# An attention tail in quarters of the array, and its sums in eight groups of rows or folded

## The chip, the cores and the metric

The kernel runs on one core of a Trainium2 chip. The metric is device time in microseconds (us) of one execution; the median of several runs is compared. A core has five engines with queues of their own: TensorE (PE; its weight loads are PEld), VectorE (DVE), ScalarE (ACT), GpSimd (POOL) and SyncE (SP), which here issues nearly all DMA transfers.

## The reference

Three blocks follow each other, over 4 sequences of 448 tokens and 768 channels. The first is attention with 12 heads of 64 channels and a soft cap of 30 on the scores:

```python
scores = cap * np.tanh(scale * q @ k.T / cap)          # 448 x 448 per head
scores = scores - np.max(scores, axis=-1, keepdims=True)
attn = np.exp(scores)
attn = attn / (np.sum(attn, axis=-1, keepdims=True) + 1e-09)
x = attn @ v
# second block, xk = mu_k * x + (1 - mu_k) * x_prev, xr likewise with mu_r
x = sigmoid(xr @ w_r) * (np.maximum(xk @ w_k, 0.0) ** 2 @ w_v)
# third block
theta = x @ w_theta
y = w_tok_r @ (x * np.cos(theta)) + w_tok_i @ (x * np.sin(theta))
u = x + y
return u + np.maximum(u @ w_ch, 0.0)
```

## The kernel before

The program has two copies of the body behind a branch on `cap`: with a cap under 64 the row maximum needs no subtraction, and this copy (`exact` false) is the one that runs. Attention goes over 24 pairs of heads (`g`), six to a sequence; the two heads of a pair lie in partitions 0 to 63 and 64 to 127. Matmuls of the weights (the second and third block) are split into three f16 matmuls of 448 columns each (high by high, high by low, low by high; lines 723 to 725, 897 to 899, 927 to 929, 949 to 951). Those of attention are f32, which the hardware runs as two records per matmul, each with a weight load of its own.

In `scores` the 448 keys of a head are taken in chunks of 128, 128, 128 and 64 (`c` = 0 to 3). For a full chunk four matmuls of 64 by 64 stand on the four quarters of the array (line 636), scores stand as keys by queries, and ScalarE makes tanh (642) and exp (646) of 896 columns, to a tile `th`. The last 64 keys of both heads are the tail: one matmul of the whole array (632) against `kd`, a 128 by 128 tile with the two heads' keys on its diagonal and zeros elsewhere, loaded by two small transfers (`diagonal`, 374); its exp is the tile `tl`, 448 columns.

In `attend` VectorE adds the three full chunks into `pz` (654). `sums` has eight matmuls of 224 columns against ones (661, 664) that put the denominators of the two heads and of the two halves of the queries into four strips of 32 rows of a PSUM tile; `den` takes the reciprocal of 224 columns (671); `spread` brings it back to 128 rows by 448 columns with two matmuls against `row` (676). `av` is the product with the values: one whole-array matmul for the tail against `vd`, values on a diagonal (680), and six of 64 columns of the array (683). ScalarE or VectorE copies it out of PSUM with a factor, VectorE multiplies by the reciprocals (688) and mixes with the token before (691 to 698), which gives the f16 operands of the next f16 matmuls.

The order on every engine is worked out ahead by a planner, `Plan.order`: a list schedule with a duration and a rank for each operation, buffers with a fixed number of slots, one queue per engine. Operations that can run on several engines carry a duration for each. At the start, `open1` makes the tiles and issues the first loads; the queries of pair 0 go on SP's queue (397), its keys on ScalarE's (398) behind the loads of `cap` and of `mu` (316, 322).

Of the kernel before, what the change touches and what calls it, by code (L numbers as in the profile page):

```python
# [7 lines left out]
F32 = mybir.dt.float32  # L8
# [12 lines left out]
NP = H // 2  # L21
# [3 lines left out]
SH = S // 2  # L25
KD = DM // 128
# [54 lines left out]
class Plan:  # L81
# [5 lines left out]
    COLS = {"av": 1.0}  # L87
    TICK = 10.24 / 3
# [58 lines left out]
    def order(self):  # L147
# [20 lines left out]
        tick, cols, warm = 0, 0.0, False  # L168
        while True:
            for e, h in ready.items():  # L170
# [81 lines left out]
def act(n):  # L252
    return 0.17 + n / 1150.0
# [19 lines left out]
def body(nc, tc, exact, qk, v, cap, mu_k, mu_r, w_k, w_v, w_r, w_th, w_tr, w_ti, w_ch, out):  # L273
# [3 lines left out]
    SLOT = 7.9  # L277
    WV0, WV1 = 190.0, 28.0
# [41 lines left out]
    mu = cpool.tile([128, 2, KD], F32, name="mu")  # L320
    for i, src in enumerate((mu_k, mu_r)):
# [3 lines left out]
    mgc = cpool.tile([128, 1], F32, name="mgc")  # L325
    nc.gpsimd.memset(mgc, MAGIC)
    unit = cpool.tile([128, 1], F32, name="unit")
    nc.gpsimd.memset(unit, 1.0)
    ones = cpool.tile([128, 3, 32], F32, name="ones")
    nc.gpsimd.memset(ones, 0.0)  # L330
    nc.gpsimd.memset(ones[:, 0], 1.0)
    nc.gpsimd.memset(ones[0:64, 1], 1.0)
    nc.gpsimd.memset(ones[64:128, 2], 1.0)
    row = cpool.tile([128, 2, 2, D], F32, name="row")
    nc.gpsimd.memset(row, 0.0)
    for h in range(2):
        for i in range(2):
            nc.gpsimd.memset(row[32 * (2 * h + i):32 * (2 * h + i) + 1, i, h], 1.0)
# [31 lines left out]
    def diagonal(e, t, src):  # L370

        for i in range(2):
            p = slice(64 * i, 64 * i + 64)
            e.dma_start(out=t[p, p], in_=src(p, i))

    def open1():
# [16 lines left out]
        qk_s.tiles = [(ra.tile([128, 2, S], F32, name=f"qk{i}"), ra.tile([128, 128], F32, name=f"kd{i}")) for i in range(qk_s.n)]  # L393
        vn_s.tiles = [(ra.tile([128, 2, KC, D], F32, name=f"vn{i}"), ra.tile([128, 128], F32, name=f"vd{i}")) for i in range(vn_s.n)]
        for _, t in qk_s.tiles + vn_s.tiles:
# [5 lines left out]
        tl_s.tiles = tiles(ra, tl_s.n, [128, S], F32, "tl")  # L401
        pz_s.tiles = tiles(ra, pz_s.n, [128, 2, S], F32, "pz")
        if exact:
            kr_s.tiles = tiles(ra, kr_s.n, [128, 2, S], F32R, "kr")
            mq_s.tiles = tiles(ra, mq_s.n, [KN, 2, 2 * KC], F32, "mq")
            mb_s.tiles = [(ra.tile([128, 2, S], F32, name=f"mb{i}"), ra.tile([128, S], F32, name=f"ml{i}")) for i in range(mb_s.n)]
        rs_s.tiles = tiles(ra, rs_s.n, [128, SH], F32, "rs")
        for t in xt_s.tiles:
            nc.gpsimd.memset(t[:, 0:1], 0.0)

    o_open1 = op("SYS", 2.0, 0, open1)
# [135 lines left out]
    tiny(3, lambda: nc.vector.tensor_scalar(out=fm.t, in0=mk.t, scalar1=-1.0, scalar2=1.0, op0=ALU.mult, op1=ALU.add), w=[fm])  # L547
    tiny(3, lambda: nc.vector.scalar_tensor_tensor(out=fa.t, in0=mk.t, scalar=-1.0, in1=mk.t, op0=ALU.mult, op1=ALU.max), w=[fa])
# [35 lines left out]
    def inputs(g):  # L584
        A = g * PAIR
        t = qkb[g] = Buf(qk_s)
        if g == 0:
            op("SYS", 3.0, A, lambda: None, w=[t], after=[o_open1], name="first")
        else:
            op("DMA", 1.3, A - 30, lambda: nc.sync.dma_start(out=t.t[0], in_=qk[g].rearrange("p (t s) -> p t s", t=2)), w=[(t, 0)], after=[o_open1], name="ldqk")  # L590
# [442 lines left out]
```

## Time and profile before

| | |
|---|---|
| median of 3 runs | 823.13 us (821.58 to 827.53) |
| the profiled execution | 822.97 us, its span in the trace 821.2 us |
| granted TensorE clock | 0.996 of full |
| TensorE busy | 791.1 us, 96% of the span |
| VectorE busy | 547.8 us, 67% |
| ScalarE busy | 439.1 us, 53% |
| GpSimd busy | 106.8 us, 13% |
| transfers | 114.73 MB, mean 140 GB/s |

Busy time of TensorE is counted from the start of a matmul to its modelled end, so it overlaps the next one's; how long a matmul holds the engine is read from the distance of two starts.

### The profile page before, as it was taken

The page shows a single profiled execution, that of the slowest core. Times are in us where ns is not written, and L with a number is a line of the kernel's source. Part 1 is how long each engine was busy: PE and PEld are TensorE (multiplying, and loading weights), DVE is VectorE, ACT ScalarE, POOL GpSimd, SP SyncE. Part 2 cuts the span into 40 slices and gives each one's busy share as a digit, 9 for nine tenths or more (in the row PEclk, how much of TensorE's full clock was granted, in tenths as well). Part 3 has the DMA queues.
Part 4 walks back from the last instruction along what each step waited for, and adds up shares of the span by engine and source line. Part 5 has one row for each costly group of instructions (what it writes and reads, how often), then busy time and mean ns, then how long its engine had stood idle before and what let it go on. Part 6 is the DMA issues. An engine that isn't in the chain of part 4 may idle for free. (4 is left out here: it accounts for less than half of the span.)

```text
span 821.2 us, 12133 instructions
## 1 busy us (share of the span) xinstructions
PE 791.1 (96%) x4586; PEld 382.0 (47%) x4586; DVE 547.8 (67%) x990; ACT 439.1 (53%) x661; POOL 106.8 (13%) x124
## 2 busy tenths in 40 slices
PE   3999999999999999999899998999999999999997
PEld 1343345444444444444455554555555555555553
DVE  1788998787666575776766877876865555545531
ACT  2898888668766666554553544444654323233201
POOL 1144223320011100111200010110401000000000
PEclk9999999999999999999999999999999999999999
DMA  6765455434533244132556887543635432434412
GB/s 207 244 197 170 154 189 196 152 125 147 165 124 127 73 137 149 49 100 75 179 174 224 289 251 235 168 145 91 136 68 108 117 81 75 93 72 98 97 38 72
DMA packets 119139, 114.73 MB, mean 140 GB/s; under 512 B 58144, under 2 KB 111136, under 8 KB 119072
## 3 DMA queue, kind: packets, MB, share of 16 engines
q1 hardware_dynamic: 117056, 113.60, 46.6%
q8 instruction: 38, 0.62, 0.3%
q10 hardware_dynamic: 2016, 0.27, 0.2%
q14 instruction: 29, 0.24, 0.1%
HBM read 78.98 MB, written 23.86 MB: 125 GB/s over the span
## 5 line engine op out<-in xcount | busy, mean ns | idle before, releaser
L642 ACT ACTIVATE th<-big,tsc 128x896 f32<-128x896 f32 x72 | 71.1, 1004 | 32.6 <-PE big L636 31.7
L646 ACT ACTIVATE th<-th,cap_t 128x896 f32<-128x896 f32 x72 | 74.1, 1040 | 0.6
L636 PE MATMUL big<-qk 64*64 64x448 f32 x576 | 70.4, 569 | 1.3 <-ACT th L642 0.8
L723 PE MATMUL one<-k,wv 128*128 128x448 f16 x192 | 68.3, 356 | 3.1 <-DVE scal L505 2.3
L723 PE MATMUL one<-sl,wk 128*128 128x448 f16 x192 | 67.9, 354 | 2.9 <-ACT g L734 2.9
L725 PE MATMUL one<-k,wv 128*128 128x448 f16 x192 | 68.3, 356 | 0.0
L724 PE MATMUL one<-k,wv 128*128 128x448 f16 x192 | 68.3, 356 | 0.0
L725 PE MATMUL one<-sl,wk 128*128 128x448 f16 x192 | 67.7, 352 | 0.0
L724 PE MATMUL one<-sl,wk 128*128 128x448 f16 x192 | 67.6, 352 | 0.0
L683 PE MATMUL one<-th,vn 128*64 128x448 f32 x288 | 59.4, 548 | 0.0
L928 PE MATMUL q<-wo,zt 128*128 128x448 f16 x168 | 59.2, 352 | 0.0
L929 PE MATMUL q<-wo,zt 128*128 128x448 f16 x168 | 59.2, 352 | 0.0
L927 PE MATMUL q<-wo,zt 128*128 128x448 f16 x168 | 59.2, 352 | 0.0
L953 ACT ACTIVATE z<-one,scal 128x448 f32<-128x448 f32 x24 | 15.1, 628 | 71.7 <-PE one L951 71.7
L698 POOL TENSOR_TENSOR sl<-mx,sl 128x448 f16<-128x448 f32 x32 | 38.5, 1206 | 99.9 <-ACT sl L288 98.2
L723 PE MATMUL one<-sl,wr 128*128 128x448 f16 x144 | 51.0, 354 | 0.0
L725 PE MATMUL one<-sl,wr 128*128 128x448 f16 x144 | 50.7, 352 | 0.0
L724 PE MATMUL one<-sl,wr 128*128 128x448 f16 x144 | 50.7, 352 | 0.0
L913 DVE SCALAR_TENSOR_TENSOR cs<-xf,scal,cs 128x896 f32<-128x896 f32 x24 | 27.6, 1150 | 30.4 <-DMA xf<-xd 24.3
L671 DVE RECIPROCAL rs<-one 128x224 f32<-128x224 f32 x24 | 37.3, 1555 | 8.9 <-PE one L664 8.6
L954 DVE TENSOR_TENSOR xf<-z,xf 128x448 f32<-128x448 f32 x24 | 15.0, 624 | 35.0 <-ACT z L953 35.0
L949 PE MATMUL one<-w_u,wc 128*128 128x448 f16 x108 | 38.1, 352 | 0.0
(182 smaller groups left out, 1674.3 us busy)
## 6 DMA issues: line engine op xcount, KB each, us to landing
qk<-in_qk SPq DMA_DIRECT2D x23, 448.0 KB, 3.5
kd<-g SPq DMA_DIRECT2D x32, 224.0 KB, 2.6
vn<-in_v SPq DMA_DIRECT2D x24, 256.0 KB, 2.8
w<-in_v SPq DMA_DIRECT2D x8, 768.0 KB, 4.6
w<-in_w_k SPq DMA_DIRECT2D x8, 768.0 KB, 5.4
w<-in_w_v SPq DMA_DIRECT2D x12, 512.0 KB, 3.8
zd<-tmp SPq DMA_DIRECT2D x24, 224.0 KB, 2.0
z<-zd SPq DMA_DIRECT2D x24, 224.0 KB, 3.2
```

The costliest lines, as they stand in the source:

```text
L636: nc.tensor.matmul(ps.t[o, h, 0:S], t.t[0][p, 1, 128 * c + 64 * i:128 * c + 64 * i + 64], t.t[0][p, 0], start=True, stop=True)
L642: op("ACT", act(n * S) + 0.08, A + 1 + 1.8 * c, lambda src=src, th=th: nc.scalar.activation(out=th.t, in_=src(), func=AF.Tanh, scale=tsc), ...
L646: op("ACT", act(n * S) + 0.08, A + 3 + 1.8 * c, lambda th=th: nc.scalar.activation(out=th.t, in_=th.t, func=AF.Exp, scale=cap_t), w=[th], ...
L683: nc.tensor.matmul(ps.t[64 * h:64 * h + 64, 0:S], vn.t[0][:, h, c], th[c].t[:, h], start=False, stop=(c == 2), skip_group_check=True)
L698: op(tt(S, True), 0, R + i, lambda e, t=t, hi=hi, lo=lo: e.tensor_tensor(out=lo.t, in0=t.t, in1=hi.t, op=ALU.subtract), r=[t, hi], w=[lo], ...
L723: nc.tensor.matmul(ps.t[:, 0:S], wh, xh(), start=(kk == 0), stop=False)
L724: nc.tensor.matmul(ps.t[:, 0:S], wh, xl(), start=False, stop=False)
L725: nc.tensor.matmul(ps.t[:, 0:S], wl, xh(), start=False, stop=(kk == len(xs) - 1))
L927: nc.tensor.matmul(o, z.t[:, 0, i], wo[i].t[:, 0], start=(i == 0), stop=False)
L928: nc.tensor.matmul(o, z.t[:, 1, i], wo[i].t[:, 0], start=False, stop=False)
L929: nc.tensor.matmul(o, z.t[:, 0, i], wo[i].t[:, 1], start=False, stop=(i == KT - 1))
L949: nc.tensor.matmul(ps.t[:, 0:S], wh, u.t[:, 0], start=(kk == 0), stop=False)
```

## The change

It has six parts.

1. The tail of the scores is four matmuls of 64 by 64 on the quarters of the array, 224 queries each; the tile `tl` then holds keys and half of the queries in its partitions, 2 heads by 224 columns. `kd` and its transfers are gone. `vd` holds the values of one half of the queries' partitions with zeros in the other, and the tail's part of `av` is four matmuls of 64 columns of the array, behind the six others.
2. For pairs under `WIDE` = 12 (`narrow`), the sums lie in eight groups of 16 rows: sixteen matmuls of 112 columns, a reciprocal of 112 columns, four spread matmuls of 112 columns.
3. For pairs from 12 on (`wide`), two additions of 64 rows (`fold`, on VectorE or POOL) put the tail into `pz`, two matmuls against ones give the sums on all 128 rows by 448 columns, the reciprocal is taken of all of these, and one operation multiplies the product, the factor and the reciprocal.
4. At the start both halves of pair 0 are issued on SP's queue, `mu` is loaded as 12 rows and turned by a matmul against the identity, a tanh of one column loads ScalarE's table early, and the fill of `kd` and `row` on POOL gives way to eight copies on VectorE.
5. The planner counts 0.09 us for each step of TensorE into or out of "qk", "av" and "sums", its estimates for these are new, and the opening operations count 1 us less each. So the whole order is made anew.
6. The copy with the row maximum changes likewise; it doesn't run here.

```diff
+    MODE = {"qk": 1, "av": 2, "sums": 3}
...
+                if e == "PE" and mode != (m := self.MODE.get(got.name, 0)):
+                    got.dur += 0.09 * ((m > 0) + (mode > 0))
+                    mode = m
...
     for i, src in enumerate((mu_k, mu_r)):
-        nc.scalar.dma_start(out=mu[:, i], in_=src.rearrange("(j p) -> p j", p=128))
+        nc.scalar.dma_start(out=mut[KD * i:KD * i + KD], in_=src.rearrange("(j p) -> j p", p=128))
...
+    nc.scalar.activation(out=warm, in_=hpi, func=AF.Tanh)
...
-        nc.sync.dma_start(out=qk_s.tiles[0][0][:, 0], in_=qk[0][:, 0:S])
-        nc.scalar.dma_start(out=qk_s.tiles[0][0][:, 1], in_=qk[0][:, S:2 * S])
-        diagonal(nc.scalar, qk_s.tiles[0][1], lambda p, i: qk[0][p, S + 384:2 * S])
+        for i in range(2):
+            nc.sync.dma_start(out=qk_s.tiles[0][:, i], in_=qk[0][:, S * i:S * i + S])
...
                 if c == 3:
-                    nc.tensor.matmul(ps.t[:, 0, 0:S], t.t[1], t.t[0][:, 0], start=True, stop=True)
+                    for h, i in ((0, 0), (1, 0), (0, 1), (1, 1)):
+                        p = slice(64 * h, 64 * h + 64)
+                        nc.tensor.matmul(ps.t[64 * i:64 * i + 64, h, 0:SH], t.t[p, 1, 384:S], t.t[p, 0, SH * i:SH * i + SH], start=True, stop=True)
...
+    def narrow(A, x, sxb, th, vn, z, sp, rs, ps):
+        def sums():
+            for k in range(2):
+                for h, i in ((0, 0), (0, 1), (1, 0), (1, 1)):
+                    c, q = 32 * (2 * h + i), SH * i + SQ * k
+                    nc.tensor.matmul(sp.t[c:c + 32, 0:SQ], ones[:, 0, k], z.t[:, h, q:q + SQ], start=(k == 0), stop=False)
+            for k in range(2):
+                for h, i in ((0, 0), (0, 1), (1, 0), (1, 1)):
+                    c = 32 * (2 * h + i)
+                    nc.tensor.matmul(sp.t[c:c + 32, 0:SQ], ones[:, 1 + i, k], th[3].t[:, h, SQ * k:SQ * k + SQ], start=False, stop=(k == 1))
...
+            nc.vector.reciprocal(out=rs.t, in_=rs.t if exact else sp.t[:, 0:SQ])
...
+            for i in range(4):
+                nc.tensor.matmul(sp.t[:, SQ * i:SQ * i + SQ], live["row"][:, i].rearrange("p h d -> p (h d)"), rs.t, start=True, stop=True)
...
+            for i in range(2):
+                for h in range(2):
+                    nc.tensor.matmul(ps.t[64 * h:64 * h + 64, SH * i:SH * i + SH], vn.t[1][:, i, h], th[3].t[:, h], start=False, stop=True, skip_group_check=True)
...
+    def wide(A, x, sxb, th, vn, z, sp, ps):
+        rs = lambda: x.t[:, 1:S + 1]
+        def sums():
+            for h in range(2):
+                nc.tensor.matmul(sp.t[64 * h:64 * h + 64, 0:S], unit.to_broadcast([128, D]), z.t[:, h], start=True, stop=True, skip_group_check=True)
...
+            nc.vector.reciprocal(out=rs(), in_=rs() if exact else sp.t[:, 0:S])
...
+            out=x.t[:, 1:S + 1], in0=ps.t[:, 0:S], scalar=sxb.t, in1=rs(), op0=ALU.mult, op1=ALU.mult), r=[ps, sxb], w=[x], name="norm"))
...
+        if g >= WIDE:
             for i in range(2):
+                p, q = slice(64 * i, 64 * i + 64), slice(SH * i, SH * i + SH)
+                op(tt(S), 0, A - 1 + 0.5 * i, lambda e, p=p, q=q: e.tensor_tensor(out=z.t[p, :, q], in0=z.t[p, :, q], in1=th[3].t[p], op=ALU.add), r=[th[3]], w=[(z, i)], name="fold")
+            wide(A, x, sx[b], th, vn, z, sp, ps)
+        else:
+            narrow(A, x, sx[b], th, vn, z, sp, rs, ps)
```

What stands on the queues is shown at three places. The first is TensorE at the very start (`big` are the PSUM tiles of the scores, `qk` the queries and keys, `one` other PSUM tiles, `w` the loaded values whose size is measured). Before:

```order
L421 MATMUL one_201<-ident,scal 128x128
L636 MATMUL big_205<-qk_266 64x448 x4
L636 MATMUL big_206<-qk_266 64x448 x4
L480 LDWEIGHTS w_228
L480 MATMUL one_201<-w_228 128x128
```

After:

```order
L651 MATMUL big_203<-qk_264 64x448 x4
L651 MATMUL big_204<-qk_264 64x448 x4
L551 MATMUL one_199<-ident,mut 128x12
L651 MATMUL big_203<-qk_264 64x448 x4
L482 LDWEIGHTS w_226
L482 MATMUL one_199<-w_226 128x128
```

The matmul that belongs to `mu` (421, now 551) moved from ahead of the first scores to behind two groups of them, and a third group stands ahead of the matmuls on `w`.

The second place is TensorE at the first pair's sums and product, with the next pair's scores around them. Before:

```order
L680 MATMUL one_198<-tl_299,vd_275 128x448
L683 MATMUL one_198<-th_291,vn_274 64x448 x2
L683 MATMUL one_198<-th_292,vn_274 64x448 x2
L683 MATMUL one_198<-th_293,vn_274 64x448 x2
L661 MATMUL one_201<-pz_302,ones 32x224 x4
L664 MATMUL one_201<-tl_299,ones 32x224 x4
L636 MATMUL big_205<-qk_268 64x448 x4
L632 MATMUL big_206<-qk_268,kd_269 128x448
L636 MATMUL big_205<-qk_270 64x448 x4
L676 MATMUL one_201<-rs_304,row 128x224 x2
```

After:

```order
L693 MATMUL one_196<-th_279,vn_268 64x448 x2
L693 MATMUL one_196<-th_280,vn_268 64x448 x2
L693 MATMUL one_196<-th_281,vn_268 64x448 x2
L696 MATMUL one_196<-tl_287,vd_269 64x224 x4
L671 MATMUL one_199<-pz_290,ones 32x112 x8
L675 MATMUL one_199<-tl_287,ones 32x112 x8
L651 MATMUL big_203<-qk_265 64x448 x4
L647 MATMUL big_204<-qk_265 64x224 x4
L687 MATMUL one_199<-rs_292,row 128x112 x4
```

The sums went from eight matmuls to sixteen of half the columns, the spread from two to four, the tail's product from one to four at the end of its group, and the tail of the scores stands here beside a score group.

The third place is VectorE at a pair of the second half: the reciprocal, and what follows it. Before:

```order
L671 RECIPROCAL rs_304<-one_201 128x224
L456 TENSOR_SCALAR w_228<-w_228 128x512
L688 TENSOR_TENSOR xt_265<-xt_265,one_201 128x448
L742 SCALAR_TENSOR_TENSOR g_222,scal<-g_222 128x448
L695 SCALAR_TENSOR_TENSOR mx_236<-mx_235,mu,xt_263 128x448
```

After, from the folds of a pair to its last product (`f` and `w` are weights on their way to f16):

```order
L740 TENSOR_TENSOR pz_290<-pz_290,tl_288 64x2x224 x2
L461 TENSOR_SCALAR f_229<-w_226 128x512
L464 SCALAR_TENSOR_TENSOR f_229<-w_226,f_229 128x512
L467 SCALAR_TENSOR_TENSOR f_229<-w_226,f_229 128x512
L713 RECIPROCAL xt_262<-one_199 128x448
L724 SCALAR_TENSOR_TENSOR xt_262<-one_196,scal,xt_262 128x448
```

Two folds stand ahead of the reciprocal, which has twice its old columns, and the product with the values is read from PSUM by the last operation instead of by a copy before it.

## Rows read from the trace of the kernel before

**Rows 1.** The page, part 1: busy us, share of span, instructions.

```profile
PE 791.1 (96%) x4586; PEld 382.0 (47%) x4586; DVE 547.8 (67%) x990; ACT 439.1 (53%) x661; POOL 106.8 (13%) x124
```

**Rows 2.** Busy time by stretches: length, busy us of each engine, clock, transfers.

```profile
0.00:20.00 20.00, 6.25 (x51) 3.02 (x52) 1.94 (x12) 4.07 (x5) 3.17 (x28) 1.00 0.63 206
20.00:50.00 30.00, 28.34 (x186) 10.51 (x186) 24.44 (x45) 27.32 (x35) 7.71 (x8) 1.00 0.73 224
50.00:100.00 50.00, 49.87 (x348) 20.03 (x347) 43.13 (x72) 44.83 (x58) 17.22 (x17) 1.00 0.57 182
...
250.00:300.00 50.00, 50.00 (x305) 21.78 (x304) 33.74 (x50) 30.71 (x46) 5.38 (x6) 1.00 0.35 110
```

**Rows 3.** Order of time, TensorE, 215 to 235 us: start, us, instruction, records.

```profile
215.42 0.50 PE L498 MATMUL one<-scal,unit 128*128 128x1 f32 x4
215.78 0.35 PE L723 MATMUL one<-sl,wk 128*128 128x448 f16 x1
...
216.16 0.35 PE L725 MATMUL one<-sl,wk 128*128 128x448 f16 x1
216.44 0.98 PE L636 MATMUL big<-qk 64*64 64x448 f32 x8
217.35 0.36 PE L723 MATMUL one<-sl,wk 128*128 128x448 f16 x1
...
221.22 0.92 PE L632 MATMUL big<-qk,kd 128*128 128x448 f32 x2
221.97 0.35 PE L723 MATMUL one<-sl,wk 128*128 128x448 f16 x1
...
229.09 0.58 PE L661 MATMUL one<-pz,ones 128*32 128x224 f32 x8
229.50 0.56 PE L664 MATMUL one<-tl,ones 128*32 128x224 f32 x8
229.99 0.36 PE L723 MATMUL one<-sl,wk 128*128 128x448 f16 x1
...
233.74 0.92 PE L676 MATMUL one<-rs,row 128*128 128x224 f32 x4
234.50 0.35 PE L723 MATMUL one<-sl,wk 128*128 128x448 f16 x1
```

**Rows 4.** The reciprocals' line: ns min/median/max, first and last start.

```profile
L671 DVE RECIPROCAL rs<-one x24: 1543/1557/1559, 28.9 to 384.0; 128x224 f32<-128x224 f32 x24
```

**Rows 5.** Groups of VectorE: busy us, mean ns, idle before and releasers.

```profile
L688 DVE TENSOR_TENSOR xt<-xt,one 128x448 f32<-128x448 f32 x24 | 14.9, 620 | 10.2 <-PE one L676 8.2 <-ACT sl L288 2.0
```

**Rows 6.** Order of time, all engines, the start (SPq: issues on SP's queue).

```profile
2.74 0.40 SPq L397 DMA_DIRECT2D qk<-in_qk  x1
...
4.19 1.43 SPq L561 DMA_DIRECT2D w<-in_v  x2
...
5.36 0.16 DVE L318 RECIPROCAL tsc<-cap_t 128x1 f32<-128x1 f32 x1 [5.36 <-DMA cap_t<-in_cap]
...
6.70 6.10 SPq L374 DMA_DIRECT2D kd<-in_qk  x2
...
14.04 3.02 PE L636 MATMUL big<-qk 64*64 64x448 f32 x16
...
15.91 1.28 ACT L642 ACT_TABLE_LOAD   x1 [15.91 <-PE big L636]
...
17.00 0.86 PE L480 MATMUL one<-w 128*128 128x128 bf16 x12
```

**Rows 7.** Transfers of the first 30 us: issues, KB each, us to landing.

```profile
w<-in_v SPq DMA_DIRECT2D x2, 768.0 KB, 7.9
...
qk<-in_qk SPq DMA_DIRECT2D x1, 224.0 KB, 3.5
qk<-in_qk ACTq DMA_DIRECT2D x1, 224.0 KB, 9.2
...
mu<-in_mu_r ACTq DMA_DIRECT2D x1, 3.0 KB, 8.9
```

More of the change, by code (lines that the diff above doesn't have):

```diff
@@ L167, in order @@
         t, seq, table, moved, locked = 0.0, 0, None, 0.0, 0.0
-        tick, cols, warm = 0, 0.0, False
+        tick, cols, warm, mode = 0, 0.0, False, 0
         while True:
@@ L368, in small @@
         return Buf(tile=scal[:, used[0] - n:used[0]])
[L370 to L374, printed above, removed]
     def open1():
@@ L600, in largest_scores @@
         mbb[g] = mb
[L601 removed]
+        op(cp(2 * S), 0, A - 2, lambda e: copy(e, kr.t, t.t), r=[t], w=[kr], name="kr")
         for j in range(KC):
@@ L616, in largest_scores, with halves @@
            r=[md[g]], w=[(mb, 0)], name="mbi")
-        op("DMA", 0.65, A + 5, lambda: nc.sync.dma_start(out=mb.t[1], in_=md[g].t.rearrange("h (o s) -> h o s", o=1).to_broadcast([2, 64, S])),
-           r=[md[g]], w=[(mb, 1)], name="rbi")
+        def halves():
+            for i in range(2):
+                nc.sync.dma_start(out=mb.t[1][64 * i:64 * i + 64], in_=md[g].t[:, SH * i:SH * i + SH].rearrange("h (o s) -> o h s", o=1).to_broadcast([64, 2, SH]))
+        op("DMA", 0.65, A + 5, halves, r=[md[g]], w=[(mb, 1)], name="rbi")
     def scores(g):
@@ new lines, in wide, with den, av @@
+    def wide(A, x, sxb, th, vn, z, sp, ps):
+        rs = lambda: x.t[:, 1:S + 1]
+        def sums():
+            for h in range(2):
+                nc.tensor.matmul(sp.t[64 * h:64 * h + 64, 0:S], unit.to_broadcast([128, D]), z.t[:, h], start=True, stop=True, skip_group_check=True)
+        op("PE", 0.74, A, sums, r=[z], w=[sp], name="sums")
+        def den():
+            if exact:
+                nc.vector.tensor_scalar(out=rs(), in0=sp.t[:, 0:S], scalar1=1e-9, scalar2=None, op0=ALU.add)
+            nc.vector.reciprocal(out=rs(), in_=rs() if exact else sp.t[:, 0:S])
+        op("DVE", 2.95, A + 1, den, r=[sp], w=[x], name="den")
+        def av():
+            for c in range(3):
+                for h in range(2):
+                    nc.tensor.matmul(ps.t[64 * h:64 * h + 64, 0:S], vn.t[0][:, h, c], th[c].t[:, h], start=(c == 0), stop=False, skip_group_check=True)
+            for i in range(2):
+                for h in range(2):
+                    nc.tensor.matmul(ps.t[64 * h:64 * h + 64, SH * i:SH * i + SH], vn.t[1][:, i, h], th[3].t[:, h], start=False, stop=True, skip_group_check=True)
+        op("PE", 3.02, A + 0.5, av, r=[vn, *th], w=[ps], name="av")
+        last1.append(op("DVE", v1(S) + 0.06, A + 4, lambda: nc.vector.scalar_tensor_tensor(
+            out=x.t[:, 1:S + 1], in0=ps.t[:, 0:S], scalar=sxb.t, in1=rs(), op0=ALU.mult, op1=ALU.mult), r=[ps, sxb], w=[x], name="norm"))
@@ L655, in attend @@
                r=[th[0], th[1]] if i == 1 else [th[i]], w=[z], name="sum")
-        def sums():
-            for h, i in ((0, 0), (0, 1), (1, 0), (1, 1)):
-                c = 32 * (2 * h + i)
-                nc.tensor.matmul(sp.t[c:c + 32, 0:SH], ones[:, 0], z.t[:, h, SH * i:SH * i + SH], start=True, stop=False)
-            for h, i in ((0, 0), (0, 1), (1, 0), (1, 1)):
-                c = 32 * (2 * h + i)
-                nc.tensor.matmul(sp.t[c:c + 32, 0:SH], ones[:, 1 + h], th[3].t[:, SH * i:SH * i + SH], start=False, stop=True)
@@ L665, in attend @@
-        op("PE", 1.1, A, sums, r=[z, th[3]], w=[sp], name="sums")
-        def den():
-            if exact:
-                nc.vector.tensor_scalar(out=rs.t, in0=sp.t[:, 0:SH], scalar1=1e-9, scalar2=None, op0=ALU.add)
-            nc.vector.reciprocal(out=rs.t, in_=rs.t if exact else sp.t[:, 0:SH])
-        op("DVE", 1.6, A + 1, den, r=[sp], w=[rs], name="den")
-        def spread():
-            for i in range(2):
-                nc.tensor.matmul(sp.t[:, SH * i:SH * i + SH], row[:, i].rearrange("p h d -> p (h d)"), rs.t, start=True, stop=True)
@@ L677, in attend @@
-        op("PE", 0.8, A + 2, spread, r=[rs], w=[sp], name="spread")
-        def av():
-            nc.tensor.matmul(ps.t[:, 0:S], vn.t[1], th[3].t, start=True, stop=False, skip_group_check=True)
-            for c in range(3):
-                for h in range(2):
-                    nc.tensor.matmul(ps.t[64 * h:64 * h + 64, 0:S], vn.t[0][:, h, c], th[c].t[:, h], start=False, stop=(c == 2), skip_group_check=True)
-        op("PE", 3.2, A + 1, av, r=[vn, *th], w=[ps], name="av")
-        x = Buf(xt_s)
```

84 lines of the change are left out of this document (53 added, 31 removed).

## The prediction

> **What bounds the kernel now.** I read the page's first part, then busy time by stretches, then TensorE in order of time. TensorE is busy for 96% of the span [rows 1]. It is short of work only in the first 20 us, 6.25 of 20; from 20 to 50 us it has 28.3 of 30, and in the later stretches it is full, 49.9 and 50.0 of 50, while VectorE has 43 of 50 from 50 to 100 us and 34 of 50 from 250 to 300 us [rows 2]. The reader should see two things in that. Time that leaves TensorE's queue, or time by which it starts sooner, comes off the end; and a VectorE at 43 of 50 has already been shown to leave TensorE its work. So the forecast is a sum over TensorE's instructions plus its start. The profiled execution took 822.97 us, 0.16 us under the median of the runs (823.13), so the sum is made against 822.97.
>
> **1. The scores' tail, 24 pairs of heads.** The old tail is one matmul of the whole array over 448 columns, 0.75 us from its start to the next instruction's (221.22 to 221.97), with no gap at either end [rows 3]. The new one is four matmuls on quarters of the array over 224 columns; four such quarters run side by side, as the 448-column score group shows (8 records in 0.91 us) [rows 3]. Half the columns is 0.375 us, so 24 × 0.375 = 9.0 us fall away. Against that stands the way in and out of the quarters. A normal score group begins 0.28 us after the f16 matmul ahead of it, where f16 matmuls follow each other at 0.19, and ends 0.91 us after its own start (216.16, 216.44, 217.35) [rows 3]: 1.00 us in all after the f16's own 0.19, against 0.75 of columns. I take the 0.25 as the price of one visit to the divided array. The order after the change has 84 unbroken runs of score matmuls where before there were 64 (17 of the 24 tails stand alone between f16 matmuls, 7 beside another score group), while the runs of sums and of A·V are 48 in both. That is 20 × 0.25 = +5.0 us. A standing-alone tail therefore wins 0.12 us only, and one beside a score group 0.37.
> The Trainium skill, TensorEngine Tiling (Array Packing), Key Properties, says that changing the tiling mode drains TensorE. The trace agrees, with the 0.25 us just read; by the columns alone, without the rule, the step would be 5.0 us better.
> The tail's A·V part is now four 64-column matmuls of 224 columns, two side by side, in place of one of 448: the same columns inside a visit that was paid for already. Zero; if they did not pair up, 24 × 0.37 = 9 us more, but the 64-column A·V matmuls beside them do so now.
>
> **2. Narrow sums, pairs 0 to 11.** Columns: before, eight matmuls of 224 over four strips; now sixteen of 112. The four strips run side by side: the first eight records lead the next by 0.41 us, the second eight the following f16 by 0.49, with the way in and out [rows 3]. Twice the records at half the columns: zero, if the columns set it. The spread back to 128 rows is now four matmuls of 112 columns (8 records) in place of two of 224 (4 records, 0.76 us from 233.74 to 234.50) [rows 3]. Each needs a fresh f32 weight load of 128 columns. What that load costs when nothing hides it is seen at matmuls of one column: four of them before the next f16 starts, 0.36 us (215.42 to 215.78) [rows 3], and as the first one's load was hidden behind the f16 matmul, some 0.11 each for the other three. 112 columns stream in 0.76/4/2 = 0.095 us. So a record costs 0.095 (hidden) to 0.11 (load-bound), 8 × 0.11 = 0.88 against 0.76: 0 to +0.12 per pair; I take the upper, as 0.11 is the longer of two overlapped things, 12 × 0.12 = +1.4 us.
> By the Trainium skill, TensorE: Matmul & The Clock Gate, LDWEIGHTS, a load takes columns over 1.2 GHz, 107 ns here; by that the estimate is +1.1 us. The rows' 0.11 decides.
>
> **3. Wide sums, pairs 12 to 23.** The tail is folded into the partial sums by two half-height additions, two matmuls of 448 columns on halves give the sums on all rows, and the spread is gone: sums' columns as before, 12 × 0.76 = −9.1 us. A·V is unchanged.
>
> **4. VectorE, ScalarE, POOL.** A reciprocal of 224 columns takes 1.557 us, of one column 0.16 [rows 4, 6]: 6.3 ns per column, so 0.86 us for 112 and 2.96 for 448. Narrow pairs give VectorE 0.7 us back; wide ones cost +1.4, and 19 of the 24 folds stand on VectorE in its order (5 on POOL), 0.62 us each by a TENSOR_TENSOR of as many columns [rows 5], +1.0 per pair; the scaling copy out of PSUM is folded into the last product. Together +2.4 us per wide pair. The 24 reciprocals start from 28.9 to 384.0 us [rows 4], one pair per 15.4 us, so 50 us hold 3.2 pairs and VectorE goes from 34 to about 41.5 of 50. That is under the 43 at which TensorE was full [rows 2], so I price it at nothing. What covers it is the queue of f16 matmuls between the sums and the next use of the PSUM tiles; without that cover each wide pair would show its reciprocal's extra 1.4 us, 17 us in all.
>
> **5. The start.** Now SP issues the first queries at 2.74 us, but the first keys go on ScalarE's queue behind two loads of mu, element by element, that land after up to 8.9 us; the keys land 9.2 us after their issue [rows 7]. SP stands at a load of the tail's keys from 6.70 for 6.1 us [rows 6]. TensorE has mu's small matmul ahead of the scores, whose first group starts at 14.04, and ScalarE loads its table at 15.91 for 1.28 [rows 6]. After: both halves lead SP's queue, mu comes in long rows and its matmul stands behind two score groups, the table load stands ahead of the scores, and the tail's key loads are gone. The second half is issued about 0.45 us after 2.74; with the 3.5 us that the queries' half needs to land [rows 7] it is there at 6.7, and as it now shares the engines with that half I take 7.2: 6.8 us sooner. Bounds: the matmuls on `w`, which hold up the rest of TensorE's queue and free the buffers for w_k, wait for two loads that are issued from 4.19 to 5.62 and land in 7.9 us [rows 6, 7], at 12.1 to 13.5, so they move up from 17.00 by 3.5 to 4.9 us; the scalar side moves by 6.8 + 1.3 = 8.1. I take the first scores' 6.8, between them, since it is they that feed ScalarE and then the whole chain, and keep 3.5 to 8.
>
> **Sum.** −9.0 + 5.0 + 1.4 − 9.1 − 6.8 = −18.5; 822.97 − 18.5 = 804.5 us.
>
> **Rivals.**
> *A, the sum holds:* 804.5; with its bounds (start 3.5 to 8, spread 0 to 1.4, a visit to the quarters at 0.2 to 0.3) 801 to 809.
> *B, the start is bound by data:* the chain through `w` sets it, or the weights behind it do, and half of the 6.8 us or more is lost, up to all of it: 808 to 811. For it: the 7.9 us that `w` takes to land; against: SP's stop of 6.1 us disappears.
> *C, VectorE becomes late in the second half:* every wide pair keeps TensorE waiting by 0.7 us, half of the reciprocal's extra: 12 × 0.7 = 8, 812.5. For it: the last product waits for the reciprocal, and the only A·V tile of PSUM for the product; against: a full pair time of f16 work lies between two uses.
> *D, the narrow sums go by records:* if each of the 32 records costs what one costs now (0.41/8 = 0.051) and not its columns, the sums take 1.64 us in place of 0.82: 12 × 0.82 = +9.8, 814. The page TensorEngine Tiling (Array Packing) of the Trainium skill, Instruction Overhead, gives each matmul some 60 cycles whatever its size, which would make it so. Against: the records' starts come in groups of four, one per strip, and a one-column record is what costs 0.11, with a load four times as wide.
> *E, slower:* the same place as C, but VectorE runs full: its queue of weight preparation and mixing falls behind and TensorE starves. To be slower by 1% it must cost 18.5 + 8.2 = 27 us over twelve pairs, 2.2 us each; VectorE would need 16 us more per 50, where 7.7 are added. 832.
>
> **Chances.** A 0.62, B 0.12, C 0.12, D 0.08, E 0.03; 0.03 for a gain beyond A, where the shorter reciprocals also close gaps of TensorE between 20 and 50 us (1.7 of 30 [rows 2]). One per cent, 8.2 us, is about what a measurement of this kernel tells from no change: faster means under 814.9. A and B lie there whole, C and D mostly: 0.88 faster, 0.09 within, 0.03 slower. For 8 in 10 the range takes A with its bounds, B and C: 799 to 814.
>
> **What would show it.** The first score group should start near 7.2 us; a tail alone should hold TensorE 0.62 us and one beside a score group 0.37; sixteen narrow sums 1.0 us with their visit, the spread 0.76 to 0.88; wide pairs should have no spread, and TensorE's idle time in front of A·V and sums there should stay near nothing. It is wrong if the gap list after 200 us names VectorE's reciprocal or its product, if the sums take 1.6 us or more, or if the weights for the first f16 matmuls land no sooner than before.

## The result, and the profile after

The changed kernel takes 811.03 us (median of four executions, 809.56 to 812.42) against 822.40 for the kernel before beside it; the ratio is 0.9849, 95% interval 0.9803 to 0.9895. Repeated on two more chips it gave 0.9841 (0.9808 to 0.9874) and 0.9839 (0.9802 to 0.9875). The mean of the three, 0.9843, is 12.9 us of 823. The forecast was 804.5 us, a gain of 18.5; the range, 799 to 814, holds the result, and "faster by over 1%" came in. Some 5.6 us of the expected gain are missing, and most of what follows asks where they are.

The profiled execution took 809.56 us, its span 807.8. The page of the changed kernel, part 1, beside [rows 1]:

```profile
PE 779.4 (96%) x4924; PEld 377.3 (47%) x4924; DVE 557.3 (69%) x1003; ACT 446.7 (55%) x676; POOL 98.0 (12%) x111
```

Busy time of the changed kernel in the stretches of [rows 2], columns as there:

```profile
0.00:20.00 20.00, 12.68 (x94) 5.39 (x96) 5.75 (x31) 11.87 (x14) 2.59 (x22) 1.00 0.80 273
20.00:50.00 30.00, 26.91 (x297) 13.37 (x295) 26.63 (x51) 26.08 (x35) 7.72 (x8) 1.00 0.75 244
50.00:100.00 50.00, 46.67 (x471) 22.58 (x467) 44.20 (x75) 44.57 (x60) 16.86 (x14) 1.00 0.50 158
100.00:150.00 50.00, 50.00 (x401) 25.49 (x398) 41.53 (x83) 41.27 (x66) 9.61 (x10) 1.00 0.57 184
...
250.00:300.00 50.00, 50.00 (x322) 19.27 (x321) 41.57 (x59) 36.27 (x54) 6.84 (x7) 1.00 0.40 128
```

[rows 2] leave out one stretch of the kernel before that belongs beside these:

```profile
100.00:150.00 50.00, 48.15 (x307) 24.48 (x310) 43.16 (x85) 38.53 (x63) 17.37 (x13) 1.00 0.54 176
```

By 20 us TensorE has done 6.4 us more than before (12.68 against 6.25; 5.5 and 5.7 more in the two repeats below): the start came sooner by nearly what was forecast. From 20 to 50 us it loses 1.4 again (26.91 against 28.34) and from 50 to 100 us another 3.2 (46.67 against 49.87). From 100 to 150 us it gains 1.85, because the kernel before was not full there; the prediction's "short of work only in the first 20 us" does not hold for that stretch, nor after 350 us (table below). From 250 to 300 us TensorE is full, and VectorE has 41.57 of 50, where 41.5 was forecast.

The waits of TensorE in the changed kernel (line waited in, line waited for, us in total, times, longest):

```profile
PE big L651 <- DMA qk<-in_qk: 7.0, 1, 7.0
PE one L778 <- DVE z L904: 4.8, 6, 1.7
PE one L687 <- DVE rs L682: 3.0, 3, 1.6
PE one L500 <- DVE scal L507: 1.7, 3, 1.1
PE one L778 <- ACT g L789: 1.7, 2, 1.3
```

L687 is the spread of the narrow sums, L682 the narrow reciprocal; the three waits stand at 23.55, 76.45 and 87.42 us. L778 are f16 matmuls and L904 a VectorE product of the phase after the pairs, from 432 us on. No wait names the wide reciprocal (L713) or the wide product (L724).

TensorE in order of time in the changed kernel, a narrow pair (165 to 180 us) and a wide one (250 to 258 us); columns as in [rows 3], to be held against it:

```profile
164.82 0.35 PE L780 MATMUL one<-sl,wr 128*128 128x448 f16 x1
165.10 0.61 PE L647 MATMUL big<-qk 64*64 64x224 f32 x8
165.64 0.36 PE L778 MATMUL one<-sl,wr 128*128 128x448 f16 x1
...
170.28 2.48 PE L693 MATMUL one<-th,vn 128*64 128x448 f32 x12
172.59 0.93 PE L696 MATMUL one<-tl,vd 128*64 128x224 f32 x8
173.45 0.36 PE L778 MATMUL one<-sl,wr 128*128 128x448 f16 x1
...
174.12 0.59 PE L671 MATMUL one<-pz,ones 128*32 128x112 f32 x16
174.53 0.57 PE L675 MATMUL one<-tl,ones 128*32 128x112 f32 x16
175.03 0.36 PE L778 MATMUL one<-sl,wr 128*128 128x448 f16 x1
```

```profile
256.07 0.35 PE L780 MATMUL one<-sl,wr 128*128 128x448 f16 x1
256.35 0.97 PE L707 MATMUL one<-pz,unit 128*64 128x448 f32 x4
257.26 0.36 PE L778 MATMUL one<-sl,wr 128*128 128x448 f16 x1
```

A lone tail holds TensorE from 165.10 to 165.64, 0.54 us, and is entered 0.28 us after the f16 matmul ahead of it where f16 matmuls follow each other at 0.19: 0.63 us in all, forecast 0.62. One beside a score group adds 0.38, forecast 0.37. Sixteen narrow sums take 0.91 plus the same 0.09, forecast 1.0; the wide sums as much. The spread's eight records take 0.88 us (median of those that f16 matmuls follow). The order holds 84 unbroken runs of scores. So the instruction terms stand: −17.9 us of columns (24 tails at 0.376 and 12 spreads at 0.757, less 0.2 because all sums take 0.01 longer), +5.2 for 20 more visits at 0.26, +1.45 for the narrow spreads, −11.25 in place of the forecast's −11.7 (−9.0 + 5.0 + 1.4 − 9.1). The busy time of TensorE bears this out: from 791.1 us [rows 1] it falls to 779.4, and to 778.1 and 778.8 in the two repeats, a little of it by the clock (0.996 in the profile before, 0.998 to 0.999 in these).

What is left is idle time. Length less TensorE's busy time, from the same view over three stretches (what runs at a lower clock counts as busy):

| TensorE idle, us | 0 to 150 | 150 to 350 | 350 to 550 |
|---|---|---|---|
| before | 17.41 | 0.00 | 6.59 |
| changed, first profile | 13.74 | 0.00 | 8.93 |
| changed, second chip | 14.73 | 0.00 | 6.30 |
| changed, third chip | 14.86 | 0.00 | 8.27 |

Up to 150 us, waiting for the first scores included, the change saves 14.44 − 17.41 = −3.0 us (mean of three profiles) where step 5 said −6.8. After 350 us it loses 1.2 on the mean, with 2.6 between profiles. Together −11.25 − 3.0 + 1.2 = −13.0, and the ratios say −12.9.

That these two meet to 0.1 us is chance, since the runs differ in one more thing. Over the 51 executions of the kernel before that stand beside the experiments the granted clock is 0.9944 on the mean, over the 17 of the changed kernel 0.9978. A line fitted through both, with one slope, gives 0.84 us for each 0.001 of clock and 10.8 us between the kernels at one clock, where their means differ by 13.6. So some 2.8 us of the gain go with the clock (an estimate from these runs), and the forecast has no term for it.

### The profile page after: what moved, and what is told of

Its sections match the earlier page's. It is cut to its first block, busy times and chain, and to the rows that moved or that the text cites. A ratio compares the mean times of both kernels' runs of the same rounds, so it can differ in the third digit from the quotient of the medians.

```text
span 807.8 us, 12787 instructions
## 1 busy us (share of the span) xinstructions
PE 779.4 (96%) x4924; PEld 377.3 (47%) x4924; DVE 557.3 (69%) x1003; ACT 446.7 (55%) x676; POOL 98.0 (12%) x111
## 4 chain that ended last, share of the span: by engine, by line
PE 82%; DMA 8%; DVE 5%; ACT 3%; issue 1%; SPq 0%; POOL 0%; DVEq 0%; POOLq 0%; ACTq 0%
PE one L778 11%; PE one L780 10%; PE one L779 10%; PE big L651 6%; PE q L984 4%; PE q L983 4%; PE q L982 4%; PE one L719 4%; PE one L1006 3%; PE one L1004 3%; PE one L1005 3%; PE q L952 2%; PE q L954 2%; PE q L953 2%; DMA ka<-kd 2%; PE one L693 2%
## 5 line engine op out<-in xcount | busy, mean ns | idle before, releaser
L778 PE MATMUL one<-k,wv 128*128 128x448 f16 x192 | 67.6, 352 | 4.9 <-DVE z L904 4.8
L778 PE MATMUL one<-sl,wk 128*128 128x448 f16 x192 | 68.1, 355 | 1.7 <-ACT g L789 1.7
L778 PE MATMUL one<-sl,wr 128*128 128x448 f16 x144 | 51.1, 355 | 0.3 <-DVE tmp L298 0.2
L454 ACT ACTIVATE w<-w 128x768 f32<-128x768 f32 (+2 forms) x32 | 26.6, 836 | 39.4 <-DMA w<-in_w_ch 16.0
L753 POOL TENSOR_TENSOR sl<-mx,sl 128x448 f16<-128x448 f32 x29 | 33.5, 1159 | 110.8 <-ACT sl L294 84.5
L713 DVE RECIPROCAL xt<-one 128x448 f32<-128x448 f32 x12 | 35.5, 2959 | 8.9 <-PE one L707 8.8
L959 ACT ACTIVATE cs<-q,scal 128x448 f32<-128x448 f32 x16 | 10.1, 632 | 53.5 <-PE q L954 53.5
L986 DVE SCALAR_TENSOR_TENSOR xf<-q,scal,xf 128x448 f32<-128x448 f32 x24 | 16.4, 683 | 33.3 <-PE q L984 33.2
```

The lines of the kernel that those rows point to most:

```text
L713: nc.vector.reciprocal(out=rs(), in_=rs() if exact else sp.t[:, 0:S])
L753: op(tt(S, True), 0, R + i, lambda e, t=t, hi=hi, lo=lo: e.tensor_tensor(out=lo.t, in0=t.t, in1=hi.t, op=ALU.subtract), r=[t, hi], w=[lo], ...
L778: nc.tensor.matmul(ps.t[:, 0:S], wh, xh(), start=(kk == 0), stop=False)
```

## Experiments

Theory T: the instruction ledger holds, and the start's gain is partly given back before 100 us. Its rivals for the giving back are R1, the reciprocals (TensorE's waits name VectorE), and R2, weights that land late. The kernel before ran beside each group of runs on the same chip: 825.02, 824.42 and 825.00 us. All kernels but the last two keep the changed kernel's order in every queue, save for what their diffs show. The diffs are shortened; "..." stands for lines left out.

### The changed kernel again, twice

> The changed kernel once more, as the base for the other runs on this chip: 811 us, 0.985 of the kernel before. Ledger theory (TensorE's own instruction time and its start set the end, and the 4.6 us that are missing from the forecast are waits of TensorE in two places, at narrow spreads and in the value phase): the same waits in the same places. Rival (the missing part is run-to-run noise): the waits stand elsewhere or are gone.

> The changed kernel once more, as the base for the three runs beside it. Ratio to the kernel before 0.981 to 0.989; TensorE's waits for VectorE in their places again: some 3 us in three early spreads, 3 to 5 us ahead of the value phase's matmuls.

811.22 us and 808.94 us. In the first of these profiles the waits stand at the same places:

```profile
PE big L651 <- DMA qk<-in_qk: 7.7, 1, 7.7
PE one L687 <- DVE rs L682: 3.2, 3, 1.6
PE one L778 <- DVE z L904: 3.2, 5, 1.6
```

The three waits at the spread belong to the kernel; those ahead of L778 vary (3.2 to 4.8).

### The tail back on the whole array

```diff
-for h, i in ((0, 0), (1, 0), (0, 1), (1, 1)):
-    nc.tensor.matmul(ps.t[64*i:64*i+64, h, 0:SH], t.t[p, 1, 384:S], t.t[p, 0, SH*i:SH*i+SH], ...)
+nc.tensor.matmul(ps.t[:, 0, 0:S], t.t[1], t.t[0][:, 0], start=True, stop=True)
 ...
-nc.tensor.matmul(ps.t[64*h:64*h+64, SH*i:SH*i+SH], vn.t[1][:, i, h], th[3].t[:, h], ...)
+nc.tensor.matmul(ps.t[:, 0:S], vn.t[1], th[3].t, start=True, ...)
```

with the block-diagonal tiles for the tail's keys and values, and their small loads, as before the change.

> The tail of the scores and its A·V part go back to one whole-array matmul each with keys and values on a diagonal; everything else and the order of all operations stay. Ledger theory: 17 tails that stand alone go from 0.637 us to 0.752 (+2.0) and 7 beside a score group from 0.376 to 0.752 (+2.6), A·V the same: +4.6, about 815.6 us. Rival 1 (the way into and out of the quarters eats the gain): within 1 us of the changed kernel. Rival 2 (the 46 small key loads, back on SP's queue, delay others): +8 or more, with new waits for loads.

819.61 us, ratio 0.9933 (0.9910 to 0.9955): +8.4 us on the changed kernel beside it. The ledger expected +4.6; the time is rival 2's, and ScalarE's waits for loads of w_k in the first 100 us rise from 4.7 to 8.2 us with the small loads back. On TensorE a whole-array tail between f16 matmuls takes 0.75 us, the columns add 9.0 and 17 visits fewer save 4.5, so +4.5 by instructions, as step 1 has it. The rest is idle time, 16.22 us up to 150 against 14.73, and a granted clock of 0.97 in each of the first two stretches of 50 us. So step 1's −4.0 is read from how long the instructions hold TensorE; this run's time does not part it from what the small loads cost, which the forecast did not count.

### Narrow sums in four strips of 224 columns

```diff
-for k in range(2): ...  nc.tensor.matmul(sp.t[c:c+32, 0:SQ], ones[:, 0, k], z.t[:, h, q:q+SQ], ...)
+nc.tensor.matmul(sp.t[c:c+32, 0:SH], strip[:, 0], z.t[:, h, SH*i:SH*i+SH], start=True, stop=False)
 ...
-nc.vector.reciprocal(out=rs.t, in_=sp.t[:, 0:SQ])
+nc.vector.reciprocal(out=rs.t, in_=sp.t[:, 0:SH])
 ...
-for i in range(4):   # spread
+for i in range(2):
```

> Narrow pairs get the four strips of 224 columns back (eight matmuls, a reciprocal of 224 columns, two spread matmuls); the quarters, the wide pairs and the order of all operations stay. Ledger theory by instructions alone: sums the same, spread 0.757 us in place of 0.877, 12 times: -1.4, about 809.6 us. Theory that TensorE waits for VectorE at the narrow spreads (3.0 us in three of them in the changed kernel): each reciprocal takes 0.7 us longer, so up to 12 x 0.7 = 8.4 us more waiting at the spreads, and 811 to 818 us; the spreads' waits tell them apart.

813.35 us, ratio 0.9858 (0.9824 to 0.9892): 2.1 us above the changed kernel's median, with overlapping intervals, although it has 1.4 us less of spread. That lies in the range of the second theory, waits for VectorE (811 to 818). In its profile the waits at the spread are twice as long:

```profile
PE one L690 <- DVE rs L685: 6.1, 4, 2.3
```

and TensorE's idle time up to 150 us is 17.39, against 14.73. So what the eight groups bring they bring through the reciprocal of 112 columns (0.848 us in place of 1.549), in the first 150 us, and it is about 3 us in these profiles; on TensorE they cost 1.4. By the runs' times the net gain of 2.1 is not clear of their scatter.

### The start's loads as before

```diff
-nc.sync.dma_start(out=qk_s.tiles[0][:, i], in_=qk[0][:, S*i:S*i+S])       # both halves
+nc.sync.dma_start(out=qk_s.tiles[0][:, 0], in_=qk[0][:, 0:S])
+nc.scalar.dma_start(out=qk_s.tiles[0][:, 1], in_=qk[0][:, S:2*S])          # behind mu
 ...
-nc.scalar.dma_start(out=mut[KD*i:KD*i+KD], in_=src.rearrange("(j p) -> j p", p=128))
+nc.scalar.dma_start(out=mu[:, i], in_=src.rearrange("(j p) -> p j", p=128))
 ...
-nc.scalar.activation(out=warm, in_=hpi, func=AF.Tanh)
```

> The first keys go back to ScalarE's queue behind two element-by-element loads of mu, and the early table load goes; the order of all operations stays. Ledger theory: the first scores start near 13.2 us in place of 7.0 and all is 6 to 7 us later, 817 to 818 us. Rival (the start is bound by the values and weights, whose loads stand on SP's queue in both): the first TensorE work on w moves less than 4 us, and the time by no more than that, 813 to 815 us.

817.17 us, ratio 0.9916 (0.9889 to 0.9943): +6.0 us, where the ledger expected 6 to 7 and the rival 2 to 4. The first scores start at 12.73 us in place of 7.0 to 7.7 (the tail's key loads stay gone, so this is not the whole old start). The lateness stays as it is to the end. The first f16 matmul and the wide reciprocals (first and last start), with the old loads and then in the changed kernel:

```profile
42.75 0.36 PE L776 MATMUL one<-sl,wk 128*128 128x448 f16 x1
...
L711 DVE RECIPROCAL xt<-one x12: 2952/2959/2960, 200.3 to 376.0; 128x448 f32<-128x448 f32 x12
```

```profile
35.86 0.36 PE L778 MATMUL one<-sl,wk 128*128 128x448 f16 x1
...
L713 DVE RECIPROCAL xt<-one x12: 2952/2959/2962, 193.7 to 369.4; 128x448 f32<-128x448 f32 x12
```

That is 6.9 us at the first f16 matmul and 6.6 at both reciprocals. In the kernel before the first f16 matmul stood where it stands with the old loads:

```profile
42.94 0.36 PE L723 MATMUL one<-sl,wk 128*128 128x448 f16 x1
```

So the loads are worth nearly what step 5 said, and their lead is not given back, against the second half of theory T. TensorE's idle time up to 150 us is then 18.95, more than the 17.41 of the kernel before: with the old loads the new order does worse there than the old order did. And from 50 to 100 us TensorE is idle for 4.6 us without the early start too:

```profile
50.00:100.00 50.00, 45.42 (x461) 22.14 (x460) 44.65 (x75) 44.53 (x60) 18.00 (x15) 1.00 0.53 167
```

In the three profiles of the changed kernel it is 3.1 to 3.4 us there, in the kernel before 0.13. So these waits came with the rest of the change and not with the sooner start.

### Reciprocals left out: wide, narrow, both

```diff
-nc.vector.reciprocal(out=rs(), in_=sp.t[:, 0:S])                 # wide: first and third kernel
+nc.vector.tensor_scalar(out=rs(), in0=sp.t[:, 0:S], scalar1=2.0 ** -9, scalar2=None, op0=ALU.min)
-nc.vector.reciprocal(out=rs.t, in_=sp.t[:, 0:SQ])                # narrow: second and third
+nc.vector.tensor_scalar(out=rs.t, in0=sp.t[:, 0:SQ], scalar1=2.0 ** -9, scalar2=None, op0=ALU.min)
```

> The changed kernel with the reciprocal of the twelve wide pairs left out: a minimum with a constant takes its place, 448 columns, so about 0.6 us in place of 2.96, which takes 12 times 2.3 = 28 us from VectorE between 200 and 400 us; every queue keeps its order. The theory on record (VectorE has room there, the queue of f16 matmuls covers its reciprocal): no gain between 100 and 350 us, since TensorE's idle time there is already 0.2 to 0.5 us in 50; 0 to -1 us in all. The theory that VectorE work is pushed back by the wide pairs and surfaces in the value phase, where TensorE waits 3 to 5 us for products of VectorE: these waits shrink, -2 to -5 us. The rival that the wide reciprocals themselves hold TensorE: -8 us or more.

> The changed kernel with the reciprocal of the twelve narrow pairs left out: a minimum with a constant on the same 112 columns takes its place, about 0.2 us in place of 0.85, every queue in its old order. If the three early spreads wait for the reciprocal's own length, each wait of 0.7 to 1.6 us shortens by 0.65 us: -2 us in all, with the waits at the spread 1 to 1.5 us and not 3. If they wait because VectorE comes to the sums late (work ahead of the reciprocal in its queue), the waits stay near 3 us and the time within 0.6 us. More than -4 us would mean that VectorE is full in the first 100 us and each microsecond there is worth a part of one at the end.

> Both kinds of reciprocal left out as in the two kernels beside this one (a minimum with a constant in their place), order kept: the most that any cheaper reciprocal can bring. If VectorE's lateness is the whole of TensorE's added idle time, the time falls by 4 to 7 us against the changed kernel. If the added idle time comes from elsewhere (loads at the start, ScalarE's activations, the order itself), by less than 2 us.

810.99, 810.05 and 809.92 us, beside 808.94 for the changed kernel; ratios 0.9851, 0.9823 and 0.9836 against 0.9839. Nothing moved. That takes rival C out: 28 us less of VectorE in the wide pairs is worth nothing, the reciprocal is wholly covered. It also takes out R1 as far as the reciprocals' length goes, and the idea that the wide pairs push VectorE's work into the value phase: with the wide reciprocals gone, the waits for L904 were 5.0 us. VectorE in order of time shows why a shorter reciprocal does not help the early spread. The kernel without narrow reciprocals:

```profile
74.46 1.78 DVE L467 SCALAR_TENSOR_TENSOR f<-w,f 128x768 uint32<-128x768 uint32 x1
...
76.17 0.26 DVE L682 TENSOR_SCALAR rs<-one 128x112 f32<-128x112 f32 x1
...
76.49 0.97 PEld L687 LDWEIGHTS one<-rs,row 128*128 128x128 f32 x8 [1.40 <-DVE rs L682]
76.49 1.15 PE L687 MATMUL one<-rs,row 128*128 128x112 f32 x8 [1.00 <-DVE rs L682]
```

The sums had left TensorE by 74.12, but VectorE was in a step of the weights' preparation until 76.2. TensorE still waits 1.0 us for an operation of 0.26. The waits at the spread fell from 3.1 to 1.8 and 2.1 us in the two kernels without narrow reciprocals, but TensorE's idle time up to 150 us is 13.70 and 14.07 there, against 13.74 to 14.86 in the table: what this wait gives back does not show in the whole.

### Weights that land sooner

```diff
-def ld(w=w, a=a):
+def ld(w=w, a=a, u=128 if early else 256):
...
-    in_=src[n*a:n*a+n, 256*m:256*m+256]
+    in_=src[n*a:n*a+n, 256*m:256*m+u]
```

The second kernel has this too, halves its first two loads of v in the same way, and fills what they leave with zeros on VectorE in the first 5 us.

> The changed kernel in its own order; the eight loads of w_k bring only half of each row (the other half of the buffer keeps what lay there), so half of w_k's data is left out and each load moves 384 KB in place of 768. In the changed kernel ScalarE stands 2.9 + 3.8 us at these loads in the first 100 us, against 0 + 1.3 us before the change, while TensorE is idle for 12 us there. If the start gives back its gain because the weights are late (the forecast's rival B), ScalarE's waits fall under 2 us and the time by 2 to 4 us against the changed kernel (ratio to the kernel before about 0.980 where the changed kernel has 0.984). If the early waits come from the order in VectorE's and ScalarE's queues, the time stays within 1 us.

> As the run beside it, and the first two loads of v on which the scale of x rests bring only half as well (the rest of those buffers is zeros; the scale is then that of half of v). They land at 12 to 14 us now and hold up the first f16 matmuls' chain. If the start is bound by this chain, the first matmul on these loads starts 2 to 4 us sooner than at 12 us and the time falls by a further 2 to 4 us. If the chain of scores, tanh, exp and sums sets the start, nothing further.

810.19 us, ratio 0.9822 (0.9790 to 0.9854), and 808.53 us, ratio 0.9813 (0.9778 to 0.9847). ScalarE's waits for loads in the first 100 us, in the changed kernel and then in the one with halved w_k:

```profile
ACT w L454 <- DMA w<-in_w_k: 5.7, 3, 2.8
...
ACT w L454 <- DMA w<-in_w_r: 1.5, 1, 1.5
```

```profile
ACT w L454 <- DMA w<-in_w_r: 1.5, 1, 1.5
ACT w L454 <- DMA w<-in_w_k: 1.5, 1, 1.5
```

The lateness went (5.7 to 1.5 us), and of TensorE's idle time up to 150 us about 1 us with it (13.40 and 13.45 against 14.44, where the three profiles of the changed kernel lie between 13.74 and 14.86). By the ratios, against the mean 0.9843, it is 1.7 and 2.5 us; the changed kernel did not run on this chip, and the intervals overlap. That is between the two expectations (2 to 4 us, and within 1). From 50 to 100 us TensorE is still idle for 2.4 and 2.6 us. The matmuls on the halved loads of v start at 12.64 us, not sooner than 12.39: here and in the changed kernel they follow straight on a score group, so these loads did not hold them up. R2 is a part of the loss, 1 us of TensorE's waits and by the ratios perhaps 2.5, and not the whole.

### All pairs wide, all pairs narrow

```diff
-    WIDE = 12
+    WIDE = 0        # first kernel; 24 in the second
```

The order is planned anew in both.

> All 24 pairs with the wide sums, the order planned anew: twelve more spreads of 0.88 us leave TensorE, -10.5 us, and VectorE gets 2.4 us more in each of the first twelve pairs. The ledger with VectorE covered gives 800 us. With VectorE at 44 of 50 us between 50 and 100 us already, some 3 pairs per 50 us add 7: more than it has, so TensorE waits; the early stretches lose about what the spreads give, 805 to 820.

> All 24 pairs with the narrow sums, the order planned anew: twelve spreads of 0.88 us come back to TensorE in stretches where it has no idle time, +10.5 us against the changed kernel: 820 to 822 us, ratio to the kernel before about 0.997. If TensorE's instructions in the second half were not what bounds, the time would stay within 2 us of the changed kernel's.

All wide: 838.42 us, ratio 1.0175 (1.0138 to 1.0212), slower than before the change and than the 805 to 820 expected. All narrow: 826.97 us, ratio 1.0036 (1.0009 to 1.0063), 5 us above what was expected. Busy time of the all-wide kernel in two stretches, columns as in [rows 2]:

```profile
50.00:100.00 50.00, 36.86 (x212) 13.77 (x214) 40.98 (x55) 27.09 (x34) 18.56 (x16) 0.76 0.31 97
100.00:150.00 50.00, 38.30 (x236) 15.68 (x232) 43.71 (x68) 35.02 (x51) 12.86 (x11) 0.83 0.46 149
```

and its waits of TensorE from 50 to 150 us:

```profile
PE big L651 <- ACT th L657: 7.7, 3, 3.8
PE one L707 <- DVE pz L740: 4.4, 1, 4.4
PE one L488 <- DVE junk L486: 3.1, 2, 2.4
PE one L707 <- DVE xt L713: 2.6, 1, 2.6
```

This is much like rival E, in the place where the change does not put it. With folds and long reciprocals in the first twelve pairs too, TensorE is idle for 25 of 100 us; VectorE has 41.0 and 43.7 of 50, about the 43.13 of [rows 2] at which TensorE was full. A busy share under a level that was once harmless did not protect it. Most of the waits name VectorE, but the largest names ScalarE, which is far from full (27.1 and 35.0 of 50) and itself stands 10.7 us at loads of w_r there; how much of this is VectorE's work alone is not shown. Nor is idle time the whole cost: at a clock of 0.965 to 0.976 in its runs, some 20 of the 27 us above the changed kernel go with the clock (an estimate, by the 0.84 us for each 0.001). All narrow costs 12 × 0.877 = 10.5 us of spreads in stretches where TensorE is full, plus two stretches at the lower clock in its profile (about 3 us, last section) and 2.6 us more idle time after 350 us (10.41 against 7.83); 826.97 stands 16 to 18 us above the changed kernel. So the split, not either form of sums, carries the gain of step 3: wide sums in the second half, where they make TensorE wait for nothing, and narrow ones in the first, where wide ones leave it idle.

No kernel here is faster than the changed one by more than the intervals leave open.

## Why the prediction was right or wrong, point by point

- **Step 1, the tail (−9.0 + 5.0): right.** 0.63 us alone (0.62 forecast), 84 runs, and +4.5 us of instructions when it is undone (of +8.4 in time). The Trainium skill, TensorEngine Tiling (Array Packing), Key Properties, says that a change of tiling mode drains TensorE; the trace agrees with 0.09 us going in and some 0.17 coming out.
- **Step 2, the spread (+1.4): right,** 0.88 us against 0.757. Rival D (32 records at a fixed price each) is out: 32 records took 0.91 us, the four strips' records start 7 ns apart, and the next four 0.096 us later, which is the time of their columns (0.095 in the prediction). The page that the prediction names for rival D, TensorEngine Tiling (Array Packing) of the Trainium skill, Instruction Overhead, gives a matmul of one column the time of one of 60; at 112 columns the trace shows nothing on top of the columns.
- **Step 3 (−9.1): right,** and shown from the other side by the all-narrow kernel's 10.5 us of spreads.
- **Step 4 (0 on VectorE): right where it was reckoned,** the second half: 41.57 of 50 from 250 to 300 us, no wait on wide reciprocals, and nothing gained without them. Its parts were less exact: a fold took 0.76 us on VectorE, not 0.62. The reason given was too weak: "under the 43 at which TensorE was full" did not hold in the all-wide kernel, nor in the changed one from 50 to 100 us, where VectorE at 44.20 left TensorE idle for 3.3 us and VectorE at 42.1 (both reciprocals out) still for 3.1.
- **Step 5 (−6.8): right in the main.** The first scores moved by 7.0 us (14.04 to 7.01; forecast near 7.2), the first f16 matmul by 7.1 (42.94 to 35.86), and undoing the loads costs 6.0 us. The first load of w_k is issued 4.6 us sooner (17.89 to 13.28), so the sign that would have spoken against the step did not show.
- **From 20 to 100 us: the term that the forecast put at nothing.** "What bounds the kernel now" took a VectorE at 43 of 50 as shown to leave TensorE its work. In the new order TensorE waits 4.8 us more there than before (mean of three profiles: 1.6 up to 50 us and 3.2 after), and waits 1.85 us less from 100 to 150. That, and a start that is worth 5.9 by 20 us in place of 6.8, makes −3.0 in place of −6.8. The time is rival B's, 808 to 811, but not for B's reason: the sooner start is not lost, and weights that land sooner bring back 1 us of waits, perhaps 2.5 in time.
- **The value phase:** the forecast had no term for it; TensorE's idle time after 350 us is 1.2 us longer on the mean. With 6.3 to 8.9 in three profiles of one kernel, that is within what varies.

The sum as measured: −11.25 − 3.0 + 1.2 = −13.0, against −18.5. Of the 5.5 us between them 3.8 lie before 150 us, 1.2 in the value phase, 0.45 in the instructions. The clock, with which some 2.8 us of the gain go, is in neither sum; at one clock the kernels differ by some 10.8 us, and 7.7 are missing.

**What stays open.** Why TensorE waits from 20 to 100 us is shown only in part. Taking back one part at a time, and keeping the new order, leaves it idle from 50 to 100 us for 4.6 us (old loads), 3.3 (tail on the whole array), 4.9 (four strips), 3.0 and 3.1 (no narrow reciprocal) and 2.4 and 2.6 (half the weights), against 0.13 in the one profile of the kernel before. So none of these parts alone makes the waits. What all these kernels share is the order that the planner made anew; VectorE has 42 to 45 of 50 us in them there and ScalarE 41 to 45; the new forms in the old order, or another order of these two queues, did not run, so that the order is the cause is not shown.

## What to carry to other kernels

In these runs a lead at the first instruction came through whole: with the old loads everything behind was 6 to 7 us later. What was lost was lost apart from it, and a run that takes the lead away and keeps the order tells the two apart. When a change also has the order planned anew, the stretch just after the start, with engines that are nearly full, needs a term of its own in the forecast. A step that trades TensorE time for VectorE time pays stage by stage: the same edit gained 16 us in the second half (all narrow against the changed kernel) and lost 27 in the first (all wide against it), each with the order planned anew and in part by the clock; busy shares alone did not tell which, waits did. Taking out a wait that the trace names, without the work standing ahead of its releaser, may move nothing.

## What the runs showed of the hardware

Records on parts of the array have no large fixed price: a tail of four quarters of 224 columns (0.54 us), a strip group of 32 records of 112 (0.91) and a group of eight of 448 on quarters (0.91) all take their columns over the parts that work side by side, plus the way in (0.09) and out (0.17). After a gap of TensorE the granted clock can fall to its lower level of 1.2 GHz for some microseconds. TensorE in order of time, the kernel before, then the all-narrow kernel:

```profile
496.57 0.35 PE L899 MATMUL q<-xs,wt 128*128 128x448 f16 x1
499.19 0.36 PE L723 MATMUL one<-k,wv 128*128 128x448 f16 x1 [2.27 <-DVE scal L505]
...
501.69 0.58 PE L724 MATMUL one<-k,wv 128*128 128x448 f16 x1
502.06 0.58 PE L725 MATMUL one<-k,wv 128*128 128x448 f16 x1
```

```profile
504.43 0.53 PE L778 MATMUL one<-k,wv 128*128 128x448 f16 x1 [2.94 <-DVE z L904]
504.75 0.58 PE L779 MATMUL one<-k,wv 128*128 128x448 f16 x1
...
507.68 0.35 PE L778 MATMUL one<-k,wv 128*128 128x448 f16 x1
507.87 0.35 PE L779 MATMUL one<-k,wv 128*128 128x448 f16 x1
```

Matmuls of 448 columns start 0.37 us apart there, 0.19 elsewhere, and one such stretch cost about 1.5 us. In the all-narrow kernel the clock is low at the first matmul behind the gap, in the kernel before some 2 us after it. The three profiles of the changed kernel have no such stretch and others of the same order have one; in the all-wide kernel, with gaps of 1.8 to 4.4 us, the granted clock was 0.76 from 50 to 100 us. The Trainium skill, TensorE: Matmul & The Clock Gate, Part 1: The HAM clock gate, says that an idle TensorE is gated to half its clock; the trace agrees. So a gap of TensorE such as these (2.27 and 2.94 us) can cost more than its own length. The spread between executions of one kernel (up to 10.7 us among 23 of the kernel before) goes with the clock: of its 51 executions beside the experiments the 17 at 0.996 and more have a median of 821.3 us, the 34 below that 825.4. Where in each run the clock fell was not recorded.
